# Weight stores moved from POOL to SP, half tiles without zero columns, twelve jobs with undivided scores, decay copies on ScalarE

## The chip, the core and the metric

The kernel runs on one core of one Trainium2 chip. The metric is device microseconds of one execution; the runs of the kernel before took 1110.32 to 1112.38 us, median 1110.91. The engines are TensorE (PE; its weight loads are shown as PEld), VectorE (DVE), ScalarE (ACT), GpSimd (POOL) and SyncE (SP), which issues most DMAs. Each engine works through its own queue in order.

## The reference

An attention with decay over 4 batches and 8 heads (576 positions, 64 columns per head), then two feed-forward layers (512 to 2048 to 512 columns) over the 2304 positions. Cut to what is computed:

```
scores = q @ k^T / sqrt(64)
cum    = cumsum(log(clip(f, 1e-4, 1)))
scores = where(causal, -1e9, scores + cum[:, None] - cum[None, :])
attn   = exp(scores - max) ; attn /= sum(attn) + 1e-9
x      = attn @ v                       # heads side by side: 2304 x 512
x      = (h * clip(h + 3, 0, 6) / 6) @ w_out1,  h = x @ w_in1
out    = where(h >= 1, h, where(h <= -1, 0, (h + 1)^2 / 4)) @ w_out2,  h = x @ w_in2
```

## The kernel before

The feed-forward layers go over 9 blocks of 256 positions per layer and 16 chunks of 128 hidden columns per block; one step of the list `steps` is one chunk of one block, 288 steps in all. `moe_h` makes the hidden columns of a step, `moe_o` (two steps later) adds them to the block's result in PSUM. Every operand is divided into a rounded part and a rest, and each product takes three matmuls.

Attention lies beside the first 112 steps. Its work is cut into jobs: 16 pairs of heads over the first 256 positions (kind "two", two heads in one job) and 16 pairs over the last 320 (two jobs of kind "one", one per head with two tiles of 128 rows, and one job "last": the half tiles of 64 rows of both heads, put together in one tile of 128). The jobs of three batches' first halves come first (12 jobs "two"). `u_load` issues a job's loads two jobs ahead (keys `kraw`, queries `qraw`, decay rows `dec`), `u_split` makes the masked decay `dm` on POOL and divides keys and queries, `u_scores` makes scores and softmax, `u_norm` and `u_trans` scale and transpose the probabilities, `u_out` multiplies by v. The first `NATS` = 8 jobs are taken undivided: their loads go straight into `kn` and `qn`, and each score is one f32 matmul. The first `DECS` = 3 jobs get their decay rows from a matmul in PSUM (`dc`) that is copied into `dec`.

Weights come as raw 64-bit words (`wraw`, four buffers). `w_split` takes half a chunk in five instructions: ScalarE's absolute value (line 175), then VectorE's lines 176, 180, 183 and 186 into `wr`. In layer 1 the result is divided into a resident buffer; for layer 2 (steps 38 to 106) it is stored to DRAM (`wf<-wr`, line 191, from POOL) for later. `wr` has two buffers, and the result of a finished block (`osb`, line 611) takes its buffers from the same tag.

The program is written in a planned order (`goal` from the costs in `seq`, `weights_until(g)` at each step); a scheduler then sets each engine's queue from priorities and an assumed timeline. In a tile pool a buffer is taken over when its last user is done; an instruction then waits at its place in the queue.

Of the kernel before, what the change touches and what calls it, by code (L numbers as in the profile page):

```python
# [16 lines left out]
P = 128  # L17
# [7 lines left out]
QA = 256  # L25
# [3 lines left out]
DECS = 3  # L29
NATS = 8  # L30
NORMS = 12
# [40 lines left out]
def tile_kernel(  # L72
# [88 lines left out]
    def w_split(kind, c, half, s, raw):  # L161
# [7 lines left out]
        ks = slice(4 * half, 4 * half + 4)  # L169
        r = moe.tile([P, 4, P], F32, tag="wr", name="wr", bufs=2)  # L170
        rf = r.rearrange("p k n -> p (k n)")
# [18 lines left out]
        if s is None:  # L190
            nc.gpsimd.dma_start(out=wf[c][:, ks], in_=r)
        else:
            rounded("a", wsb[s][:, 0, ks], r)
            rest("v", wsb[s][:, 1, ks], r, wsb[s][:, 0, ks])

    def w_keep(c, s):
# [31 lines left out]
    def u_load(n):  # L228
# [13 lines left out]
        if d["nat"]:  # L242

            kk = att.tile([P, S], F32, tag="kk", name="kn", bufs=3)
            qq = att.tile([P, 2 * QA], F32, tag="qh", name="qn", bufs=3)
            nc.sync.dma_start(out=kk[:, 0:nk], in_=k[b, h:h + 2, :, 0:nk].rearrange("h p n -> (h p) n"))
            for y in range(2):
                nc.sync.dma_start(
                    out=qq[y * D:(y + 1) * D, 0:nq], in_=q[b, h + y, y * D:(y + 1) * D, q0:q0 + nq]
                )  # L250
            d.update(kk=kk, qh=qq)
        else:
            kraw = att.tile([P, S], F32, tag="kraw", name="kraw", bufs=1)
            qraw = att.tile([P, 2 * QA], F32, tag="qraw", name="qraw", bufs=1)
            for y in range(2):
                nc.sync.dma_start(
                    out=kraw[y * D:(y + 1) * D, 0:nh * nk].rearrange("p (h n) -> p h n", h=nh),
                    in_=k[b, h:h + nh, :, 0:nk].rearrange("h p n -> p h n"),
                )
            if kind == "two":  # L260
                nc.sync.dma_start(
                    out=qraw.rearrange("p (h n) -> p h n", h=nh),
                    in_=q[b, h:h + nh, :, q0:q0 + nq].rearrange("h p n -> p h n"),
                )
            else:

                o = QA + W4 * (h % 2)
                nc.gpsimd.memset(qraw[:, S - o:S - o + W4], 0.0)
                nc.sync.dma_start(out=qraw[:, 0:QA], in_=q[b, h, :, q0:q0 + QA])
                nc.sync.dma_start(out=qraw[:, o:o + W4], in_=q[b, h, :, q0 + QA:S])  # L270
            d.update(kraw=kraw, qraw=qraw)
        w = nk if kind == "two" else 4 * P
        dec = att.tile([P, S], F32, tag="dec", name="dec")
        if n < DECS:
            t = bank("dc")
            for y in range(nh):
                ty = t[:, y * QA:(y + 1) * QA]
                for c in range(QA // P):
# [3 lines left out]
                    )  # L282
            rounded("v", dec[:, 0:nh * nk], t[:, 0:nh * nk])
        else:
# [8 lines left out]
    def u_split(n):  # L293
# [13 lines left out]
        else:  # L307
# [6 lines left out]
            if not d["nat"]:  # L314
# [4 lines left out]
                ql = att.tile([P, 2 * QA], F32R, tag="ql", name="ql", bufs=3)  # L319
                w, x = nh * d["nk"], 2 * QA if kind == "two" else QA + P  # L320
                rounded("a", kk[:, 0:w], kraw[:, 0:w])
# [8 lines left out]
    def softmax(d, z, py, pieces):  # L330

        mx, sm = d["mx"], d["sum"]
        for x, (s, dc, a, e) in enumerate(pieces):
            nc.vector.tensor_tensor_reduce(  # L334
                out=py[:, a:e], in0=s, in1=dc, scale=-0.125,
                scalar=mx[:, 2 * z:2 * z + 1] if x else 3.0e38,
                op0=ALU.add, op1=ALU.min, accum_out=mx[:, 2 * z + x:2 * z + x + 1],
            )
        x = len(pieces) - 1
# [4 lines left out]
    def u_scores(n, i):  # L344
# [5 lines left out]
        if kind == "last":  # L350
            pr = att.tile([P, S], F32, tag="prob2", name="prob2")
            d["prob"][i] = pr
            ta, tb = bank("sc"), bank("sc")
            for part in ("qh", "ql"):
                for t, a, e in ((ta, 0, 4 * P), (tb, 4 * P, S)):
                    for y in range(2):
                        o = jobs[n - 2 + y]
                        nc.tensor.matmul(
                            t[:, 0:e - a], lhsT=o[part][:, QA:QA + P], rhs=o["kk"][:, a:e],
                            start=part == "qh" and y == 0, stop=part == "ql" and y == 1,  # L360
                        )
            softmax(d, 0, pr, [(ta, dec[:, 0:4 * P], 0, 4 * P), (tb[:, 0:W4], dm[:, 0:W4], 4 * P, S)])
            return
# [23 lines left out]
        for y in range(nh):  # L387
            t, zd = ts[y], y * 2 + j
            pieces = [(t[:, 0:w0], dec[:, y * nk:y * nk + w0], 0, w0)] if w0 else []
            pieces.append((t[:, w0:width], dm[:, zd * P:(zd + 1) * P], w0, width))  # L390
            softmax(d, zd, pr[:, y * width:(y + 1) * width], pieces)
# [186 lines left out]
    def moe_o(g):  # L578
# [30 lines left out]
        if n == NCH - 1:  # L609
            for k in range(2):  # L610
                o = moe.tile([P, 512], F32, tag="wr", name="osb", bufs=2)
                scale = 1.0 / 6.0 if layer == 0 else 1.0
# [69 lines left out]
    for n, c in enumerate(first):  # L682
        t = PRE0 + (PRE1 - PRE0) * n // NCH
        wq += [(t - 3, t, "raw", c, half, None) for half in range(2)]
    wq.sort(key=lambda x: x[0])
# [7 lines left out]

    def weights_until(t):
        weights_ahead(t)
        while any(x[1] <= t for x, _ in pend):
# [9 lines left out]

    upper = att.tile([P, QA], F32, tag="upper", name="upper", bufs=1)
    nc.gpsimd.memset(upper, 1.0)
# [122 lines left out]
```

## Time and profile before

| | |
|---|---|
| median of 3 runs | 1110.91 us (1110.32 to 1112.38) |
| profiled execution | 1115.45 us, of which the span of instructions is 1113.7 us |
| busy in the span | PE 1048.2, PEld 947.3, DVE 635.4, ACT 512.6, POOL 138.4 us |
| mean granted TensorE clock | 0.964 of 2.4 GHz |
| instructions | 20349 |
| DMA | 144.35 MB, mean 130 GB/s |

Attention and the weight splits end near 557 us; what comes after is feed-forward work alone. A busy share over the whole span therefore mixes stages with different limits, and the rows below are cut by stage.

### The profile page before, as it was taken

The numbers are of one execution on the slowest core, as the hardware profiler recorded it, in microseconds if no ns is written. First come the engines' busy times: TensorE is split into PE (matmuls) and PEld (weight loads), VectorE is DVE, ScalarE is ACT, GpSimd is POOL, SyncE is SP. The second block draws the span as 40 slices with busy tenths as digits, with TensorE's granted clock in tenths as the row PEclk, the third lists the DMA queues.
The fourth block names the chain that finished last, engine by engine and source line by source line (L and its number), as shares of the span: only waits on it lengthen the run. The fifth ranks groups of instructions, "written<-read, shape, count | busy, mean of one in ns | idle before, by whom it ended". The sixth has DMA issues, their size and how long they took to land.

```text
span 1113.7 us, 20349 instructions
## 1 busy us (share of the span) xinstructions
PE 1048.2 (94%) x7324; PEld 947.3 (85%) x7324; DVE 635.4 (57%) x1846; ACT 512.6 (46%) x1314; POOL 138.4 (12%) x335
## 2 busy tenths in 40 slices
PE   7987998969889998989999999999999999999998
PEld 4676888958789888878889999998999999999997
DVE  8999984665677777767754336532333333333232
ACT  6876754545456654545554235432223323233232
POOL 2100000111111111111000000111211212212111
PEclk8697999989999999998999999999999999999999
DMA  8965781764496595774545125310100101000000
GB/s 253 314 212 175 218 272 57 221 219 121 128 339 189 152 325 162 231 262 128 182 151 185 39 65 182 97 38 1 39 10 29 39 1 39 20 19 29 1 21 19
DMA packets 72101, 144.35 MB, mean 130 GB/s; under 512 B 11840, under 2 KB 43072, under 8 KB 67904
## 3 DMA queue, kind: packets, MB, share of 16 engines
q1 hardware_dynamic: 69440, 134.66, 38.5%
q0 software_dynamic: 2560, 8.39, 1.9%
q8 instruction: 57, 0.93, 0.4%
q14 instruction: 44, 0.36, 0.1%
HBM read 116.74 MB, written 26.29 MB: 128 GB/s over the span
## 4 chain that ended last, share of the span: by engine, by line
PE 70%; DMA 14%; DVE 9%; issue 4%; ACT 2%; SPq 0%; POOL 0%; ACTq 0%; DVEq 0%; POOLq 0%
PE hp L552 31%; PE o L604 18%; PE o L597 12%; DMA dec<-ncum 5%; PE av L466 3%; PE pt L424 3%; DMA wf<-wr 2%; PE sc L383 2%; DMA qraw<-in_q 2%; DMA wraw<-in_w 2%; DVE prob L334 2%; DMA kraw<-in_k 1%; DMA x2d<-osb 1%; DMA w<-wf 1%; DVE wr L183 1%
## 5 line engine op out<-in xcount | busy, mean ns | idle before, releaser
L597 PE MATMUL o<-g,w 128*128 128x256 f32 x1728 | 254.1, 293 | 22.3 <-ACT g L118 18.8
L597 PEld LDWEIGHTS o<-g,w 128*128 128x128 f32 x1728 | 228.5, 195 | 31.9 <-ACT g L118 22.1
L552 PE MATMUL hp<-xt,w 128*128 128x256 f32 x1728 | 249.4, 291 | 4.9 <-ACT w L118 3.6
L552 PEld LDWEIGHTS hp<-x,w 128*128 128x128 f32 x1728 | 227.3, 191 | 12.8
L552 PEld LDWEIGHTS hp<-xt,w 128*128 128x128 f32 x1728 | 226.3, 194 | 11.3 <-ACT w L118 4.4
L552 PE MATMUL hp<-x,w 128*128 128x256 f32 x1728 | 231.8, 283 | 0.0
L604 PE MATMUL o<-w,g 128*128 128x512 f32 x864 | 224.9, 395 | 0.0
L126 DVE TENSOR_TENSOR g<-u,g 128x256 fp32r<-128x256 f32 x288 | 123.4, 430 | 106.0 <-POOL g L120 86.8
L561 ACT ACTIVATE u<-hp 128x256 f32<-128x256 f32 x144 | 55.4, 386 | 267.9 <-PE hp L552 264.9
L604 PEld LDWEIGHTS o<-w,g 128*128 128x128 f32 x864 | 152.6, 189 | 25.4
L563 DVE SCALAR_TENSOR_TENSOR u<-hp,u 128x256 f32<-128x256 f32 x144 | 60.7, 423 | 157.4 <-ACT u L562 157.4
L120 POOL TENSOR_SCALAR g<-u 128x256 fp32r<-128x256 f32 x144 | 58.7, 408 | 399.5 <-PE o L604 242.2
L340 ACT ACTIVATE prob<-prob,mx 128x256 f32<-128x256 f32 (+4 forms) x144 | 83.5, 581 | 35.9 <-DVE mx L334 35.2
L559 DVE SCALAR_TENSOR_TENSOR u<-u,hp 128x256 f32<-128x256 f32 x144 | 59.5, 416 | 57.2 <-ACT u L558 57.0
L558 ACT ACTIVATE u<-hp 128x256 f32<-128x256 f32 x144 | 54.0, 379 | 79.7 <-PE hp L552 79.1
L424 PE MATMUL pt<-ident,prob 128*128 128x128 f32 (+1 forms) x400 | 68.6, 292 | 22.4 <-DVE prob L409 18.2
L118 ACT ACTIVATE g<-u 128x256 fp32r<-128x256 f32 x144 | 59.0, 413 | 36.4 <-DVE u L559 35.7
L424 PEld LDWEIGHTS pt<-ident,prob 128*128 128x128 f32 (+1 forms) x400 | 49.1, 148 | 28.8 <-issue 11.4
L118 ACT ACTIVATE pt<-pt 128x512 f32<-128x512 f32 (+3 forms) x160 | 61.5, 433 | 22.1 <-PE pt L424 21.9
L175 ACT ACTIVATE wr<-wraw 128x512 f32<-128x512 f32 x64 | 43.2, 674 | 49.3 <-DMA wf<-wr 25.8
L334 DVE CUSTOM_DVE_ANT_0 prob<-sc,dec 128x128 f32<-128x128 f32 (+3 forms) x112 | 50.8, 457 | 24.6 <-PE sc L383 15.9
L562 ACT ACTIVATE u<-u 128x256 f32<-128x256 f32 x144 | 60.2, 420 | 4.4
(72 smaller groups left out, 954.0 us busy)
## 6 DMA issues: line engine op xcount, KB each, us to landing
wraw<-in_w SPq DMA_DIRECT2D x64, 512.0 KB, 9.7
w<-wf SPq DMA_DIRECT2D x24, 1024.0 KB, 8.9
dec<-ncum SPq DMA_DIRECT2D x45, 256.0 KB, 7.0
kraw<-in_k SPq DMA_DIRECT2D x64, 144.0 KB, 5.7
wf<-w SPq DMA_DIRECT2D x8, 1024.0 KB
wf<-wr POOLq DMA_DIRECT2D x32, 256.0 KB, 6.2
w<-wf SPq DMA_DIRECT2D x16, 512.0 KB, 3.5
vv<-in_v SPq DMA_DIRECT2D x16, 320.0 KB, 5.4
```

Source lines behind the costliest of these rows:

```text
L118: nc.scalar.activation(out=out, in_=in_, func=AF.Copy)
L120: nc.gpsimd.tensor_scalar(out=out, in0=in_, scalar1=1.0, scalar2=1.0, op0=ALU.mult, op1=ALU.mult)
L126: e.tensor_tensor(out=out, in0=in_, in1=hi.bitcast(F32), op=ALU.subtract)
L334: nc.vector.tensor_tensor_reduce(out=py[:, a:e], in0=s, in1=dc, scale=-0.125, scalar=mx[:, 2 * z:2 * z + 1] if x else 3.0e38, op0=ALU.add, ...
L340: nc.scalar.activation(out=py, in_=py, func=AF.Exp, scale=-1.0, bias=mx[:, 2 * z + x:2 * z + x + 1], accum_out=sm[:, z:z + 1],)
L424: nc.tensor.transpose(t[:nk, o:o + P], p[:, c:c + nk], ident)
L552: nc.tensor.matmul(hp, lhsT=ws[:, a, k], rhs=x[:, bb], start=(k == 0 and a == 0 and bb == 0), stop=(k == KD - 1 and bb == 1),)
L559: nc.vector.scalar_tensor_tensor(out=u, in0=u, scalar=6.0, in1=hp, op0=ALU.min, op1=ALU.mult)
L562: nc.scalar.activation(out=u, in_=u, func=AF.Square)
L563: nc.vector.scalar_tensor_tensor(out=u, in0=hp, scalar=1.0, in1=u, op0=ALU.max, op1=ALU.min)
L597: nc.tensor.matmul(o, lhsT=ws[:, a, KD + k], rhs=gg[:, bb], start=False, stop=(n == NCH - 1 and bb == 1 and k % 2 == 1),)
L604: nc.tensor.matmul(acc[j][k], lhsT=gg[:, bb, k * P:(k + 1) * P], rhs=ws[:, a, KD:2 * KD].rearrange("p k n -> p (k n)"), start=(n == 0 and ...
```

## The change

Stores of split weights are collected in a list and issued by SP at the start of the next step (`w_store`); the raw loads of layer 2 may go out six steps ahead of their split, not three; `wr` has three buffers. Twelve jobs are undivided, not eight. The copy of the decay rows from PSUM is ScalarE's. The queries of a job "one" are loaded in one piece of 320 columns; the zero columns that stood beside the half tiles, and POOL's memset for them, are gone. Instead the scores of the two half tiles are made in separate PSUM areas, the first with 64 rows, the second with 128 of which the upper 64 are used, in three banks, and the softmax's maximum pass runs once per half. The constant `upper` shares the buffer of `kraw`.

```
-NATS = 8
+NATS = 12
...
-        r = moe.tile([P, 4, P], F32, tag="wr", name="wr", bufs=2)
+        r = moe.tile([P, 4, P], F32, tag="wr", name="wr", bufs=3)
...
         if s is None:
-            nc.gpsimd.dma_start(out=wf[c][:, ks], in_=r)
+            stores.append((wf[c][:, ks], r))
...
+    def w_store():
+        for out_, r in stores:
+            nc.sync.dma_start(out=out_, in_=r)
+        stores.clear()
...
-            if kind == "two":
-                nc.sync.dma_start(
-                    out=qraw.rearrange("p (h n) -> p h n", h=nh),
-                    in_=q[b, h:h + nh, :, q0:q0 + nq].rearrange("h p n -> p h n"),
-                )
-            else:
-                o = QA + W4 * (h % 2)
-                nc.gpsimd.memset(qraw[:, S - o:S - o + W4], 0.0)
-                nc.sync.dma_start(out=qraw[:, 0:QA], in_=q[b, h, :, q0:q0 + QA])
-                nc.sync.dma_start(out=qraw[:, o:o + W4], in_=q[b, h, :, q0 + QA:S])
+            nc.sync.dma_start(
+                out=qraw[:, 0:nh * nq].rearrange("p (h n) -> p h n", h=nh),
+                in_=q[b, h:h + nh, :, q0:q0 + nq].rearrange("h p n -> p h n"),
+            )
...
-            rounded("v", dec[:, 0:nh * nk], t[:, 0:nh * nk])
+            rounded("a", dec[:, 0:nh * nk], t[:, 0:nh * nk])
...
-                w, x = nh * d["nk"], 2 * QA if kind == "two" else QA + P
+                w, x = nh * d["nk"], nh * d["nq"]
...
+        for x, piece in enumerate(pieces):
+            for s, dc, a, e, y in piece:
+                rs = slice(0, P) if y is None else slice(y * D, y * D + D)
+                nc.vector.tensor_tensor_reduce(
+                    out=py[rs, a:e], in0=s, in1=dc, scale=-0.125,
...
-            ta, tb = bank("sc"), bank("sc")
+            ta, tc_, tb = bank("sc"), bank("sc"), bank("sc")
+            tt = [[ta, tb[:, 0:W4]], [tc_, tb[:, P:P + W4]]]
+            for y in range(2):
+                o = jobs[n - 2 + y]
+                for part in ("qh", "ql"):
+                    for x, (a, e) in enumerate(((0, 4 * P), (4 * P, S))):
+                        m = D if y == 0 else P
                         nc.tensor.matmul(
-                            t[:, 0:e - a], lhsT=o[part][:, QA:QA + P], rhs=o["kk"][:, a:e],
+                            tt[y][x][:m, 0:e - a], lhsT=o[part][:, QA + W4 - m:QA + W4], rhs=o["kk"][:, a:e],
...
-        wq += [(t - 3, t, "raw", c, half, None) for half in range(2)]
+        wq += [(t - 6, t, "raw", c, half, None) for half in range(2)]
...
     def weights_until(t):
+        w_store()
         weights_ahead(t)
```

Where instructions now stand is shown at three places, all around the first stores of layer 2's weights. First POOL's queue before; `wf` is the store of a split, `dm<-dec` a mask over decay rows, `qraw` the memset of zero columns.

```order
L268 MEMSET qraw 128x64
L191 DMA wf_98<-wr 128x512
L299 AFFINE_SELECT dm<-dec 128x64
L303 AFFINE_SELECT dm<-dec 64x64
L191 DMA wf_98<-wr 128x512
L191 DMA wf_99<-wr 128x512
L309 AFFINE_SELECT dm<-dec 128x256
L268 MEMSET qraw 128x64
L191 DMA wf_99<-wr 128x512
```

POOL's queue now, in the same part of the program:

```order
L309 AFFINE_SELECT dm<-dec 128x256 x2
L299 AFFINE_SELECT dm<-dec 128x64
L303 AFFINE_SELECT dm<-dec 64x64
L309 AFFINE_SELECT dm<-dec 128x256 x2
L299 AFFINE_SELECT dm<-dec 128x64
L303 AFFINE_SELECT dm<-dec 64x64
```

The masks alone are left; before, the second store stood behind two masks, and masks behind stores. Second, SP's queue before at that place (`w<-wf` reloads a chunk's weights, `wraw` loads raw words):

```order
L618 DMA x2d<-osb 128x2x256 x2
L256 DMA kraw<-in_k 64x576 x2
L157 DMA w_118<-wf_85 128x2048
L236 DMA dec<-ncum 128x1x576
L223 DMA vv<-in_v 128x2x320
L154 DMA wraw<-in_w 128x1024 x2
L157 DMA w_117<-wf_84 128x2048
L285 DMA dec<-ncum 128x512
```

SP's queue now:

```order
L626 DMA x2d<-osb 128x2x256
L157 DMA w_118<-wf_85 128x2048
L200 DMA wf_98<-wr 128x512
L154 DMA wraw<-in_w 128x1024
L200 DMA wf_98<-wr 128x512
L154 DMA wraw<-in_w 128x1024
L243 DMA dec<-ncum 128x1x576
L230 DMA vv<-in_v 128x2x320
L200 DMA wf_99<-wr 128x512
L157 DMA w_117<-wf_84 128x2048
L154 DMA wraw<-in_w 128x1024
```

The stores stand each ahead of a raw load, and the decay rows have moved behind two such pairs. Third, ScalarE's queue before; the number behind `wr` tells one use of a buffer from another, and with two buffers `wr_3267` takes over that of `wr_2998`.

```order
L175 ACTIVATE wr_2998<-wraw_2785 128x512
L175 ACTIVATE wr_3005<-wraw_2787 128x512
L118 ACTIVATE g_2672<-u_2669 128x256
L340 ACTIVATE prob1_2678,sum_2560<-prob1_2678,mx_2561 128x512
L340 ACTIVATE prob0_2710,sum_2648<-prob0_2710,mx_2649 128x384
L558 ACTIVATE u_2743<-hp_2730 128x256
L118 ACTIVATE xt_2760<-av_2749 128x256
L118 ACTIVATE g_2746<-u_2743 128x256
L558 ACTIVATE u_2802<-hp_2789 128x256
L118 ACTIVATE xt_2763<-av_2749 128x64
L118 ACTIVATE g_2805<-u_2802 128x256
L175 ACTIVATE wr_3267<-wraw_3076 128x512
```

ScalarE's queue now; with three buffers, two of which last held a block's result (`osb`), `wr_3233` takes over that of `wr_2955`.

```order
L622 ACTIVATE osb_2669<-o1_1441 128x512
L175 ACTIVATE wr_2955<-wraw_2545 128x512
L175 ACTIVATE wr_2965<-wraw_2547 128x512
L342 ACTIVATE prob0_2592,sum_2520<-prob0_2592,mx_2521 128x384
L175 ACTIVATE wr_3225<-wraw_2793 128x512
L118 ACTIVATE pt_2409<-pt_2612 128x8x64
L566 ACTIVATE u_2631<-hp_2618 128x256
L566 ACTIVATE u_2705<-hp_2692 128x256
L118 ACTIVATE pt4_2410<-pt_2637 64x128
L118 ACTIVATE g_2634<-u_2631 128x256
L175 ACTIVATE wr_3233<-wraw_2961 128x512
```

Three splits stand directly behind the block's result, and the fourth, the first that waits for a store, has eight rows between it and the first; before, the third had ten.

## Rows read from the trace of the kernel before

**Rows 1.** The page: busy time of TensorE, its share of the span, instructions.

```profile
PE 1048.2 (94%) x7324; PEld 947.3 (85%) x7324; DVE 635.4 (57%) x1846; ACT 512.6 (46%) x1314; POOL 138.4 (12%) x335
```

**Rows 2.** Stretches: length, busy time of PE, PEld, DVE, ACT, POOL, clock, DMA, GB/s.

```profile
20.00:105.00 85.00, 71.67 (x433) 56.04 (x431) 81.93 (x267) 66.93 (x182) 7.09 (x10) 0.80 0.79 251
105.00:197.00 92.00, 83.88 (x641) 77.94 (x642) 68.09 (x202) 53.24 (x134) 4.82 (x14) 0.96 0.55 176
...
219.70:240.00 20.30, 10.11 (x68) 9.93 (x67) 9.91 (x30) 6.30 (x18) 3.06 (x7) 0.75 0.76 252
...
298.00:317.00 19.00, 12.38 (x67) 11.38 (x66) 12.77 (x38) 7.61 (x20) 3.24 (x8) 0.82 0.76 289
...
498.00:512.00 14.00, 9.89 (x47) 9.00 (x46) 10.31 (x30) 6.82 (x16) 3.66 (x9) 0.63 0.42 131
...
557.00:700.00 143.00, 143.00 (x1162) 137.06 (x1161) 69.20 (x172) 60.68 (x144) 5.79 (x16) 1.00 0.39 125
```

**Rows 3.** Waits, 197 to 557 us: who, for whom, total us, times, longest.

```profile
POOL dm L299 <- DMA dec<-ncum: 87.7, 9, 13.4
...
ACT wr L175 <- DMA wf<-wr: 25.8, 8, 7.6
...
ACT wr L175 <- DMA x2d<-osb: 11.3, 5, 5.1
```

**Rows 4.** ScalarE in order of time, 218.5 to 236 us: start, duration, [idle before].

```profile
219.37 0.42 ACT L118 ACTIVATE g<-u 128x256 fp32r<-128x256 f32 x1
227.37 0.66 ACT L175 ACTIVATE wr<-wraw 128x512 f32<-128x512 f32 x1 [7.57 <-DMA wf<-wr]
```

**Rows 5.** TensorE in order of time, 218.5 to 236 us.

```profile
221.22 2.08 PE L597 MATMUL o<-g,w 128*128 128x256 f32 x16
233.49 0.66 PE L424 MATMUL pt<-ident,prob 128*128 128x128 f32 x2 [10.19 <-DVE prob L409]
```

**Rows 6.** POOL in order of time, 205 to 232 us.

```profile
219.06 0.23 POOL L299 TENSOR_SCALAR_AFFINE_SELECT dm<-dec 128x64 f32<-128x64 f32 x1 [7.59 <-DMA dec<-ncum]
219.36 0.41 POOL L303 TENSOR_SCALAR_AFFINE_SELECT dm<-dec 64x64 f32<-64x64 f32 x1
219.73 0.56 POOL L191 DMA_DIRECT2D wf<-wr  x1
```

**Rows 7.** Waits of SP's queue, 197 to 557 us.

```profile
SPq L154 <- DVE wr L186: 45.0, 16, 9.2
```

**Rows 8.** DMA issues: out<-in, engine, count, KB each, median us to landing.

```profile
wf<-wr POOLq DMA_DIRECT2D x32, 256.0 KB, 6.2
...
x2d<-osb SPq DMA_DIRECT2D x18, 256.0 KB, 3.7
```

**Rows 9.** Groups by shape, VectorE, 20 to 105 us: count | busy us, mean ns.

```profile
L126 DVE TENSOR_TENSOR kk<-kraw,kk 64x512 fp32r<-64x512 f32 x4 | 2.8, 690 | 0.1
L126 DVE TENSOR_TENSOR ql<-qraw,qh 128x512 fp32r<-128x512 f32 x4 | 2.7, 687 | 0.0
```

**Rows 10.** Groups by shape, whole span, VectorE and ScalarE.

```profile
L118 ACT ACTIVATE pt<-pt 128x512 f32<-128x512 f32 x64 | 37.8, 592 | 16.8 <-PE pt L424 16.6
...
L334 DVE DVE_READ_ACCUMULATOR2_ANT mx<- 128x1 f32 x256 | 21.0, 82 | 0.0
...
L126 DVE TENSOR_TENSOR ql<-qraw,qh 128x384 fp32r<-128x384 f32 x32 | 17.9, 560 | 15.8 <-ACT qh L118 15.6
...
L334 DVE CUSTOM_DVE_ANT_0 prob<-sc,dec 128x512 f32<-128x512 f32 x16 | 11.0, 687 | 7.8 <-DMA dec<-ncum 6.6 <-PE sc L358 1.1
...
L334 DVE CUSTOM_DVE_ANT_0 prob<-sc,dm,mx 128x64 f32<-128x64 f32 x16 | 4.5, 279 | 0.3 <-PE sc L358 0.2
...
L122 DVE COPY dec<-dc 128x512 f32<-128x512 f32 x3 | 2.1, 685 | 1.4 <-PE dc L279 1.4
```

**Rows 11.** Groups by shape, whole span, TensorE.

```profile
L373 PE MATMUL sc<-kn,qn 64*128 64x256 f32 x32 | 11.2, 533 | 1.6 <-ACT pt L118 0.8 <-DVE mx L334 0.7
...
L383 PE MATMUL sc<-kk,qh 128*128 128x256 f32 x16 | 4.6, 308 | 0.0
```

More of the change, by code (lines that the diff above doesn't have):

```diff
@@ L194, in w_split @@
             rest("v", wsb[s][:, 1, ks], r, wsb[s][:, 0, ks])
+    stores = []
+    def w_store():
+        for out_, r in stores:
+            nc.sync.dma_start(out=out_, in_=r)
+        stores.clear()
     def w_keep(c, s):
@@ L332, in softmax @@
         mx, sm = d["mx"], d["sum"]
[L333 to L338, printed above, removed]
+        for x, piece in enumerate(pieces):
[3 more added lines that the diff above has]
+                    out=py[rs, a:e], in0=s, in1=dc, scale=-0.125,
+                    scalar=mx[rs, 2 * z:2 * z + 1] if x else 3.0e38,
+                    op0=ALU.add, op1=ALU.min, accum_out=mx[rs, 2 * z + x:2 * z + x + 1],
+                )
         x = len(pieces) - 1
@@ L352, in u_scores @@
             d["prob"][i] = pr
-            ta, tb = bank("sc"), bank("sc")
[L354 to L357, printed above, removed]
+            ta, tc_, tb = bank("sc"), bank("sc"), bank("sc")
[5 more added lines that the diff above has]
+                        m = D if y == 0 else P
                         nc.tensor.matmul(
-                            t[:, 0:e - a], lhsT=o[part][:, QA:QA + P], rhs=o["kk"][:, a:e],
-                            start=part == "qh" and y == 0, stop=part == "ql" and y == 1,
-                        )
-            softmax(d, 0, pr, [(ta, dec[:, 0:4 * P], 0, 4 * P), (tb[:, 0:W4], dm[:, 0:W4], 4 * P, S)])
+                            tt[y][x][:m, 0:e - a], lhsT=o[part][:, QA + W4 - m:QA + W4], rhs=o["kk"][:, a:e],
+                            start=part == "qh", stop=part == "ql",
+                        )
+            softmax(d, 0, pr, [
+                [(tt[y][0][y * D:y * D + D], dec[y * D:y * D + D, 0:4 * P], 0, 4 * P, y) for y in range(2)],
+                [(tt[y][1][y * D:y * D + D], dm[y * D:y * D + D, 0:W4], 4 * P, S, y) for y in range(2)],
+            ])
             return
@@ L388, in u_scores @@
             t, zd = ts[y], y * 2 + j
-            pieces = [(t[:, 0:w0], dec[:, y * nk:y * nk + w0], 0, w0)] if w0 else []
-            pieces.append((t[:, w0:width], dm[:, zd * P:(zd + 1) * P], w0, width))
+            pieces = [[(t[:, 0:w0], dec[:, y * nk:y * nk + w0], 0, w0, None)]] if w0 else []
+            pieces.append([(t[:, w0:width], dm[:, zd * P:(zd + 1) * P], w0, width, None)])
             softmax(d, zd, pr[:, y * width:(y + 1) * width], pieces)
@@ L610, in moe_o @@
             for k in range(2):
-                o = moe.tile([P, 512], F32, tag="wr", name="osb", bufs=2)
+                o = moe.tile([P, 512], F32, tag="wr", name="osb", bufs=3)
                 scale = 1.0 / 6.0 if layer == 0 else 1.0
@@ L704, in tile_kernel @@
     lf = att.tile([P, L], F32, tag="prob1", name="lf")
-    upper = att.tile([P, QA], F32, tag="upper", name="upper", bufs=1)
+    upper = att.tile([P, QA], F32, tag="kraw", name="upper", bufs=1)
     nc.gpsimd.memset(upper, 1.0)
```

## The prediction

> **What bounds the kernel now.** I read the stages first, then the waits, then the order of time inside the worst stretch. TensorE is busy for 94% of the span [rows 1], and from 557 us on it hardly pauses (143.00 of 143.00 us in 557:700 [rows 2]), so nothing that the change touches (attention and weight splits, all done by then) can be won there. What can be won lies before. From 20 to 105 us VectorE is the limit: 81.93 of 85 us busy against TensorE's 71.67. After that TensorE is the limit in most stretches, with holes: in the three stretches 219.7:240, 298:317 and 498:512 it is busy for 10.11 of 20.30, 12.38 of 19.00 and 9.89 of 14.00 us [rows 2]. That is 10.2 + 6.6 + 4.1 = 20.9 us of idle in 53 us, and the granted clock there is 0.75, 0.82 and 0.63, which is a mix of its two levels, 1.2 and 2.4 GHz.
>
> The waits say what they have in common [rows 3]: the first ScalarE instruction of a weight split (L175) waits for a store `wf<-wr` to land, 8 times, 25.8 us; for the store of a finished block, which shares the `wr` buffers, 5 times, 11.3 us. ScalarE runs in order, so everything behind stands too. In the worst case ScalarE stands for 7.57 us [rows 4], and TensorE follows with 10.19 us of idle [rows 5]. POOL's rows say why that store was late: it sat behind an `affine_select` that waited 7.59 us for decay rows, went out at 219.73 and freed its buffer only at 227.4 [rows 4, 6]. So the buffer is held by POOL's order as much as by the transfer.
>
> **Part 1: stores on SP, three `wr` buffers, raw loads six steps ahead.** Removed: 32 store issues from POOL and the dependence of a store on a decay transfer. Added: 32 issues on SP. They stand directly ahead of raw loads that SP already held for the same VectorE instruction (L186: 16 waits, 45.0 us [rows 7]), so the added wait mostly replaces one; what is queued behind a waiting store is a raw load, then weight reloads and decay rows. A buffer is now needed again three splits later, not two. The earlier raw loads remove nothing large, since no row of the worst waits is a wait for a raw load in this part; I set them at 0.
> Bounds: at best the three stretches lose all idle, 20.9 us, and what the low clock took, at most (1 - 0.75) x 20.30 + (1 - 0.82) x 19.00 + (1 - 0.63) x 14.00 = 13.7 us, together 34.6 us. At worst 0, if the waits move to SP's stores. My value: the first stretch goes whole, 10.2 + 5.1 = 15.3 us, since its cause is POOL's order. Of the other two, half: they also hold the wait for the block's own store, which stays. (6.6 + 3.4 + 4.1 + 5.2) / 2 = 9.7 us. Gain 25 us.
> Against it: the new ScalarE order has the splits no further apart than before (the fourth of a group needs the first one's store eight rows of the order after it was begun), so short waits stay. A store of this size took 6.2 us from POOL, and one of the same size from SP 3.7 us [rows 8]. I take the difference, 2.5 us, once for each of the five groups of splits, 12.5 us of ScalarE, half of it reaching TensorE: +6 us. Bounds 0 and the 25.8 us of now.
> A rule that speaks against this part: the Trainium skill, "DMA: Bandwidth & Descriptors", section "Queues, rings and completion order", says that a DMA engine takes turns between queue rows and works through one row's ring in order, so a store that leaves POOL's row for SP's loses its own turn and starts behind all that SP has issued. The trace so far points the other way, with 3.7 us from SP against 6.2 us from POOL [rows 8]; what the rule would make of the time is the first rival.
>
> **Part 2: twelve jobs undivided, decay rows by ScalarE.** Four jobs lose both VectorE splits, 4 x 690 + 4 x 687 ns = 5.5 us, all eight inside 20:105 [rows 9], and three copies of 685 ns leave VectorE, 2.1 us [rows 10]. Sum 7.6 us on the engine that is 96% busy there. TensorE has 13.3 us of idle in that stretch, so the gain is not capped by it; but it and ScalarE (66.93 of 85 us) are close behind, so I take 5 us. Bounds 0 (the next engine takes it all) and 7.6. The three copies cost ScalarE about 592 ns each [rows 10], beside the splits it loses; 0. TensorE swaps eight divided matmuls per job for four undivided ones, which last 533 ns for 256 columns against 308 for each of the two divided parts [rows 11]: 0, as two times 308 is no less; bounds -1 and +1 us over four jobs. Undivided scores take one bank per head; cover is the idle of TensorE just named, and without it I would add 1 us.
>
> **Part 3: half tiles without zero columns.** POOL loses 32 memsets, SP one of two query loads in each of 32 jobs, and the query splits 64 of 384 columns: VectorE 560 ns each now [rows 10], at most 32 x 560 x 64/384 = 3 us less. The price is in the softmax: each of the 16 tiles now makes four passes of 64 partitions where it made two of 128. A pass costs by its columns, not its partitions: `kk` on 64 partitions with 512 columns takes 690 ns, `ql` on 128 takes 687 [rows 9]. So 687 + 279 + 2 x 82 ns = 1.13 us more per tile [rows 10], 16 x 1.13 = 18.1 us on VectorE, between 105 and 557 us. VectorE is busy for 74% of 105:197 [rows 2], so about a quarter of it should show: (18.1 - 3) / 4 = +4 us. Bounds -3 and 18.1. These tiles also hold three score banks for longer, and the next matmul group that turns to such a bank waits. No row shows it; bounds 0 and one pass more per tile, 16 x 0.69 = 11 us; I take 2.
>
> **Part 4: SP's order.** Decay rows and key loads now stand behind stores and earlier raw loads. They wait for VectorE instructions of about the same place, so I take +2 us; bounds 0 and the third rival's price.
>
> **Sum.** -25 + 6 - 5 + 4 + 2 + 2 = -16 us. The profiled execution took 1115.45 us (span 1113.7), so about 1099.5 there. It lies 4.5 us above the median 1110.91 of the runs, so the median should come to 1095 us.
>
> **Rivals.**
> First, the stalls move: the store leaves SP promptly but lands late behind loads. With two 1 MB reloads queued and 252 GB/s in 219.7:240 [rows 2], a store lands some 8 us after its issue, more than the 7.57 us that ScalarE stood. For it: the splits stay as dense. Against it: 3.7 us [rows 8], and the third buffer. Part 1 is then worth some 5 us instead of 19: 1109 us.
> Second, the stalls go whole: 34.6 instead of 25 and no new short waits, -16 - 10 - 6 = -32 us: 1079 us. For it: 25.8 us is the whole sum of those waits. Against it: the 11.3 us for the block's store remain.
> Third, on the other side, the decay rows. POOL already waits for them 87.7 us in nine places [rows 3]. There are 16 decay loads for half tiles; if each starts behind one store and one raw load more, 768 KB at 252 GB/s, it is 3.0 us later, 48 us in all. The rest of the sum without part 4 is -18 us, so this decides from the point where three eighths of the 48 us reach TensorE; with half of it the time is -18 + 24 = +6 us, median 1117 us. For it: the new order of SP has two stores and two raw loads between a weight reload and the decay load behind it. Against it: a wait of POOL for decay rows is mostly not one of TensorE, and stores and decay loads wait for VectorE instructions that are few rows apart.
> That the change does not do what it says is excluded for the stores: the new order of POOL holds none.
>
> **How the numbers follow.** Forecast (1087 to 1104) 0.55, first rival (1104 to 1112) 0.16, second (1075 to 1087) 0.15, third (1113 to 1125) 0.14. About 0.2%, 2.2 us, is what a measurement can tell from no change, so "same" is 1108.7 to 1113.1: some half of the first rival, 0.08. Faster 0.78, slower 0.14. The range that leaves out the deeper half of the second rival and most of the third is 1079 to 1114.
>
> **What would show it.** Right: `wf<-wr` no longer ends waits of L175 for more than some 12 us in all; no TensorE idle of 10 us near 220; VectorE about 10 us busier in all (18.1 - 7.6, less the narrower splits), its busy time to 105 us less by 7.6; POOL without stores. Wrong in part 1: waits of ScalarE for the stores stay above 20 us, or TensorE's clock falls in as many stretches. Wrong in part 3: TensorE waits for VectorE's `prob` or for banks in the half tiles. Wrong in part 4: decay transfers end TensorE's idle for more than now. The prediction is wrong if the stages before 557 us do not shrink by 8 us or more.

## The result, and the profile after

The changed kernel takes 1124.72 us (median of 4 runs, 1123.12 to 1129.93), the kernel before in the same comparison 1111.64 us (1110.32 to 1113.37): a ratio of 1.0114, 95% interval 1.0082 to 1.0145. It is slower by some 13 us where the prediction had it faster by 16, and the range up to 1114 us does not hold it. The profiled execution took 1124.15 us, its span is 1122.4 us.

The page of the changed kernel answers to [rows 1]:

```profile
PE 1047.4 (93%) x7324; PEld 942.2 (84%) x7324; DVE 644.9 (57%) x1899; ACT 508.9 (45%) x1309; POOL 114.8 (10%) x271
```

TensorE's work is the same, and so is the mean granted clock (0.964 in both profiled executions), so what grew is its idle time: 1113.7 - 1048.2 = 65.5 us before, 1122.4 - 1047.4 = 75.0 us now. VectorE has 9.5 us more, about as forecast. Then the stretches of [rows 2], in the same columns, though the program now stands elsewhere in them:

```profile
20.00:105.00 85.00, 63.17 (x361) 48.83 (x362) 77.09 (x250) 59.00 (x159) 5.61 (x7) 0.74 0.75 244
105.00:197.00 92.00, 90.61 (x704) 81.67 (x703) 67.30 (x211) 56.00 (x152) 4.32 (x10) 1.00 0.53 171
219.70:240.00 20.30, 14.71 (x101) 13.67 (x100) 12.43 (x39) 7.80 (x22) 0.88 (x3) 0.92 0.97 332
298.00:317.00 19.00, 16.22 (x107) 14.45 (x106) 16.12 (x51) 9.93 (x25) 0.61 (x1) 0.82 0.99 373
498.00:512.00 14.00, 14.00 (x115) 13.59 (x114) 9.82 (x33) 7.17 (x19) 1.47 (x4) 1.00 0.49 137
557.00:700.00 143.00, 139.80 (x1125) 132.57 (x1125) 70.66 (x193) 59.01 (x145) 6.21 (x16) 1.00 0.39 128
```

In the three stretches where the prediction saw the gain, TensorE is busy for 14.71, 16.22 and 14.00 us instead of 10.11, 12.38 and 9.89: 12.5 us less idle. It was lost again elsewhere, some of it already in 20:105 (63.17 us against 71.67). Attention does not end near 557 us in either kernel, as the text ahead of the prediction and the prediction have it: its last product `av` ends at 603.0 us before and at 612.5 us now. Only the weight splits are done by then (550.7 and 552.8 us). The waits from 197 to 557 us, in the columns of [rows 3]:

```profile
POOL dm L299 <- DMA dec<-ncum: 159.0, 11, 19.5
...
ACT wr L175 <- DMA wf<-wr: 26.0, 11, 7.4
...
ACT wr L175 <- DMA x2d<-osb: 7.9, 5, 2.5
```

The splits wait for stores as long as before: 26.0 us against 25.8, in 11 waits instead of 8. The longest stands at the same place as in [rows 4]. Here is ScalarE's row of it in the changed kernel, and then SP's rows ahead of it (start, duration, instruction):

```profile
217.81 0.42 ACT L118 ACTIVATE g<-u 128x256 fp32r<-128x256 f32 x1
225.65 0.66 ACT L175 ACTIVATE wr<-wraw 128x512 f32<-128x512 f32 x1 [7.42 <-DMA wf<-wr]
```

```profile
210.70 0.40 SPq L154 DMA_DIRECT2D wraw<-in_w  x1
211.20 0.55 SPq L243 DMA_DIRECT2D dec<-ncum  x1
212.89 0.38 SPq L230 DMA_DIRECT2D vv<-in_v  x1
216.41 0.33 SPq L200 DMA_DIRECT2D wf<-wr  x1
216.82 0.38 SPq L157 DMA_DIRECT2D w<-wf  x1
```

Before, the store went out late, at 219.73 [rows 6]. Now it goes out at 216.41, and its buffer comes free 9.2 us after that, where it was 7.6 us (219.73 to 227.37). The DMA engines are busy for 0.97 of the stretch. The store stopped waiting on POOL and takes longer to land instead. TensorE's rows show what is left of the hole of 10.19 us [rows 5]:

```profile
222.97 1.20 PE L605 MATMUL o<-g,w 128*128 128x256 f32 x8
228.23 2.17 PE L560 MATMUL hp<-xt,w 128*128 128x256 f32 x9 [4.06 <-DVE u L567]
```

The DMA issues of the changed kernel, in the columns of [rows 8]:

```profile
wraw<-in_w SPq DMA_DIRECT2D x64, 512.0 KB, 8.7
...
wf<-wr SPq DMA_DIRECT2D x32, 256.0 KB, 7.5
...
x2d<-osb SPq DMA_DIRECT2D x18, 256.0 KB, 4.0
```

A store from SP lands after 7.5 us in the median, from POOL it was 6.2 [rows 8]. The kernels of the experiments below agree: 7.3 to 10.1 us in all that store from SP, 5.4 to 6.5 us in all that store from POOL. Last, VectorE's groups by shape over the whole span, which answer to [rows 10]:

```profile
L336 DVE CUSTOM_DVE_ANT_0 prob<-sc,dec 64x512 f32<-64x512 f32 x32 | 22.0, 687 | 9.7 <-DMA dec<-ncum 4.5 <-PE sc L363 4.2
...
L126 DVE TENSOR_TENSOR ql<-qraw,qh 128x320 fp32r<-128x320 f32 x32 | 15.6, 487 | 5.6 <-ACT qh L118 5.2
...
L336 DVE CUSTOM_DVE_ANT_0 prob<-sc,dm,mx 64x64 f32<-64x64 f32 x32 | 9.0, 282 | 1.8 <-issue 0.6 <-PE sc L363 0.3
...
L336 DVE DVE_READ_ACCUMULATOR2_ANT mx<- 64x1 f32 x64 | 5.0, 78 | 0.0
```

The half tiles' passes take 22.0 + 9.0 + 5.0 = 36.0 us, against 11.0 + 4.5 + 32 x 0.082 = 18.1 us before: 17.9 us more. The query splits save 2.3 us.

### The profile page after: what moved, and what is told of

Its sections match the earlier page's. It is cut to its first block, busy times and chain, and to the rows that moved or that the text cites. A ratio compares the mean times of both kernels' runs of the same rounds, so it can differ in the third digit from the quotient of the medians.

```text
span 1122.4 us, 20224 instructions
## 1 busy us (share of the span) xinstructions
PE 1047.4 (93%) x7324; PEld 942.2 (84%) x7324; DVE 644.9 (57%) x1899; ACT 508.9 (45%) x1309; POOL 114.8 (10%) x271
## 4 chain that ended last, share of the span: by engine, by line
PE 73%; DMA 11%; DVE 10%; issue 3%; ACT 2%; SPq 1%; POOL 0%; DVEq 0%; ACTq 0%; POOLq 0%
PE hp L560 33%; PE o L612 18%; PE o L605 13%; PE av L474 3%; PE pt L432 3%; DMA dec<-ncum 3%; DMA wraw<-in_w 2%; DMA wf<-wr 2%; DVE prob L336 2%; PE sc L391 2%; DMA kraw<-in_k 1%; DVE wr L186 1%; DVE wr L183 1%; PE sc L363 1%; DMA qraw<-in_q 1%
## 5 line engine op out<-in xcount | busy, mean ns | idle before, releaser
L605 PE MATMUL o<-g,w 128*128 128x256 f32 x1728 | 248.0, 288 | 19.8 <-ACT g L118 11.4
L605 PEld LDWEIGHTS o<-g,w 128*128 128x128 f32 x1728 | 223.4, 190 | 30.7 <-ACT g L118 13.7
L342 ACT ACTIVATE prob<-prob,mx 128x128 f32<-128x128 f32 (+4 forms) x144 | 83.4, 580 | 45.4 <-DVE mx L336 44.9
L336 DVE CUSTOM_DVE_ANT_0 prob<-sc,dec 128x384 f32<-128x384 f32 (+3 forms) x128 | 61.6, 486 | 28.1 <-PE sc L391 16.6
L175 ACT ACTIVATE wr<-wraw 128x512 f32<-128x512 f32 x64 | 42.7, 671 | 58.6 <-DMA wf<-wr 26.0
L309 POOL TENSOR_SCALAR_AFFINE_SELECT dm<-dec 128x256 f32<-128x256 f32 (+1 forms) x48 | 29.5, 615 | 327.4 <-DMA dec<-ncum 167.6
```

What stands on the lines that cost most here:

```text
L336: nc.vector.tensor_tensor_reduce(out=py[rs, a:e], in0=s, in1=dc, scale=-0.125, scalar=mx[rs, 2 * z:2 * z + 1] if x else 3.0e38, op0=ALU.ad ...
L342: nc.scalar.activation(out=py, in_=py, func=AF.Exp, scale=-1.0, bias=mx[:, 2 * z + x:2 * z + x + 1], accum_out=sm[:, z:z + 1],)
L605: nc.tensor.matmul(o, lhsT=ws[:, a, KD + k], rhs=gg[:, bb], start=False, stop=(n == NCH - 1 and bb == 1 and k % 2 == 1),)
```

## The experiments

Each kernel was timed beside the kernel before on the same chip; a ratio is to those runs, with its 95% interval. "Step 0" and "step 90" are the starts of the hidden products of those steps in the profile, less those of the kernel before (44.3 and 495.5 us); "end" is the same for step 144, behind all attention. The table is worked out from the traces, the columns on VectorE (busy us) and on L175 (us of waits for stores `wf`, and for raw words; the same instruction is L181 in a_s3 and h_s3) are read from them.

| kernel | median us | ratio | VectorE | L175 | step 0 | step 90 | end |
|---|---|---|---|---|---|---|---|
| changed | 1124.72 | 1.0114 [1.0082, 1.0145] | 644.9 | 26.0, 13.1 | +9.0 | +12.3 | +9.4 |
| b_half | 1114.0 | 1.0008 [0.9983, 1.0032] | 650.7 | 20.7, 6.7 | +2.1 | -2.2 | +0.2 |
| b_stores | 1111.02 | 0.998 [0.9957, 1.0002] | 636.0 | 25.2, 17.0 | +9.0 | +6.3 | -1.2 |
| b_nats_dec | 1111.28 | 0.9967 [0.9945, 0.999] | 627.4 | 26.4, 2.4 | +0.6 | -5.9 | -7.8 |
| b_upper | 1112.8 | 1.0001 [0.9969, 1.0034] | 635.3 | 26.5, 4.5 | -0.7 | +0.6 | -1.0 |
| a_nohalf | 1109.08 | 0.996 [0.9937, 0.9984] | 630.2 | 29.4, 9.8 | +8.5 | +0.6 | -3.4 |
| p_sh | 1118.24 | 1.0056 [1.0035, 1.0077] | 650.3 | 25.9, 14.8 | +8.7 | +6.9 | +2.2 |
| p_hn | 1115.4 | 1.0031 [1.0009, 1.0052] | 644.2 | 22.7, 2.5 | +1.1 | -2.2 | +2.0 |
| a_s3 | 1125.36 | 1.0137 [1.0094, 1.018] | 644.9 | 26.1, 11.7 | -0.8 | +9.6 | +10.7 |
| a_passes | 1124.91 | 1.0095 [1.0066, 1.0125] | 645.6 | 26.6, 12.4 | +11.0 | +16.2 | +11.7 |
| a_half2 | 1105.99 | 0.9926 [0.9899, 0.9954] | 626.7 | 22.7, 13.8 | +9.6 | -2.1 | -9.4 |
| b_nd_half2 | 1100.93 | 0.9889 [0.9859, 0.992] | 627.7 | 25.5, 2.1 | +1.5 | -6.7 | -14.8 |
| h_w | 1104.14 | 0.9921 [0.9898, 0.9944] | 627.0 | 19.8, 2.1 | +0.9 | -10.1 | -13.1 |
| h_pool3 | 1110.09 | 0.9966 [0.9947, 0.9984] | 627.9 | 15.8, 13.7 | +10.1 | -0.1 | -4.8 |
| h_s3 | 1104.07 | 0.9917 [0.9884, 0.9949] | 627.4 | 14.9, 10.2 | -0.9 | -7.9 | -14.3 |

### One part alone on the kernel before

b_half has the half tiles without zero columns and nothing else of the change, in its core:

```
-            ta, tb = bank("sc"), bank("sc")
+            ta, tc_, tb = bank("sc"), bank("sc"), bank("sc")
...
+            for s, dc, a, e, y in piece:
+                rs = slice(0, P) if y is None else slice(y * D, y * D + D)
```

> The kernel before with the half tiles' edit alone (queries in one piece, no zero columns, three banks, four passes of 64 partitions). Theory A (each edit has its own price, and this one is the dear one): VectorE 15 to 16 us busier than 635.4, time +8 to +12 us, 1119 to 1123. Rival B (an edit's price is that of the new queue orders, not of its work): anywhere within 1100 to 1125, with the loss not where the half tiles are. If VectorE is as much busier and the time is within 3 us of before, the passes are hidden and the loss of the whole change is elsewhere.

b_stores has the stores on SP, three buffers, the raw loads six steps ahead, and `upper` in another buffer:

```
-            nc.gpsimd.dma_start(out=wf[c][:, ks], in_=r)
+            stores.append((wf[c][:, ks], r))
...
-        wq += [(t - 3, t, "raw", c, half, None) for half in range(2)]
+        wq += [(t - 6, t, "raw", c, half, None) for half in range(2)]
```

> The kernel before with the weight stores' edit alone (SP a step later, three wr buffers, raw loads six steps ahead, upper in kraw's buffer). Theory A: the stretch from step 30 to step 54 gains 8 to 10 us as in the changed kernel, the start loses 2 to 5 us because a third split now stands before the first exponentials; 1102 to 1108. Rival C (the third buffer at the start is the whole loss): step 0 late by 7 us or more, time above 1112.

b_nats_dec is two lines:

```
-NATS = 8
+NATS = 12
...
-            rounded("v", dec[:, 0:nh * nk], t[:, 0:nh * nk])
+            rounded("a", dec[:, 0:nh * nk], t[:, 0:nh * nk])
```

> The kernel before with twelve undivided jobs and ScalarE's decay copies alone. Theory A: VectorE 7.6 us less busy, time 1104 to 1110. Rival D (these two slow the start, as the copies stand behind splits that wait for raw words): step 0 late by 5 us or more, time 1115 to 1122.

b_upper is the smallest edit of the change, as a measure of what no change looks like:

```
-    upper = att.tile([P, QA], F32, tag="upper", name="upper", bufs=1)
+    upper = att.tile([P, QA], F32, tag="kraw", name="upper", bufs=1)
```

> The kernel before with one constant (upper) in another buffer, which costs no engine any work. Theory A: within 3 us of before, 1108 to 1114. Rival B: 4 us or more away from before in either direction, since the scheduler makes another order of it.

No part alone makes the kernel slower by more than can be told from no change: +0.1%, -0.2%, -0.3% and 0.0%. Their sum would be about -0.4%, and all of them together are +1.1%. So the loss is not in one part; it appears when the parts stand together. b_half came out as the last sentence of its expectation has it: VectorE is 15.3 us busier and the time is within 3 us of before. b_stores was outside both of its ranges, and b_nats_dec just above its theory's.

The stores' part, which was to bring 19 us, brings some 2, which cannot be told from none. The two waits of the splits in b_stores go with that:

```profile
ACT wr L175 <- DMA wf<-wr: 25.2, 9, 7.1
ACT wr L175 <- DMA wraw<-in_w: 17.0, 8, 4.4
```

The waits for stores are unchanged, and waits for raw words, 4.8 us in the kernel before, have come on top.

### The change without one part, and two parts together

a_nohalf is the changed kernel with the half tiles as they were:

```
-                w, x = nh * d["nk"], nh * d["nq"]
+                w, x = nh * d["nk"], 2 * QA if kind == "two" else QA + P
...
-            ta, tc_, tb = bank("sc"), bank("sc"), bank("sc")
+            ta, tb = bank("sc"), bank("sc")
```

p_sh is the kernel before with the edits of b_stores and b_half, p_hn with those of b_nats_dec and b_half.

> The changed kernel without the half tiles' edit: the stores' edit and the twelve jobs with ScalarE's copies together. Alone these two were 0.998 and 0.997 of before. Theory A (the loss is stores and half tiles meeting: more VectorE work ahead of each store and each buffer): 1103 to 1109. Rival B (stores and the twelve jobs meet at the start, where the third split waits for raw words and the relief of VectorE is worth nothing): step 12 late by 7 us or more, 1112 to 1120.

> Stores' edit and half tiles' edit on the kernel before, eight undivided jobs, VectorE's copies. Theory A: 1119 to 1126, as the changed kernel. Rival B: the sum of the two alone, 1110 to 1114.

> Half tiles' edit and the twelve jobs with ScalarE's copies on the kernel before, stores from POOL as before. Theory A and rival B: no part of this pair meets the stores, so the sum of the two alone, 0.9975, 1108 to 1112. If it is above 1115, the loss lies between these two and the stores are innocent.

Without the half tiles the change is faster than before (0.996). The half tiles are +0.1% on the kernel before, 1.0056 - 0.998 = +0.8% beside the stores' edit, 1.0031 - 0.9967 = +0.6% beside the other edits, and 1.0114 - 0.996 = +1.5%, about 17 us, beside both. So what the half tiles cost depends on the edits beside them, also on the stores' edit, which alone makes nothing faster. The two pairs answered to neither of their theories: p_sh lies between its two ranges, and p_hn, expected at the sum of its parts, is above 1115 us, so the half tiles cost something without the stores' move too.

### The start

The changed kernel reaches step 0 9.0 us late. With three buffers, three splits stand on ScalarE ahead of the first exponentials, and the third waits for raw words. The rows of ScalarE up to the table load in front of those exponentials (start, duration, instruction, idle before), in the kernel before and then in the changed one:

```profile
9.71 0.68 ACT L175 ACTIVATE wr<-wraw 128x512 f32<-128x512 f32 x1 [0.59 <-DMA wraw<-in_w]
10.41 1.28 ACT L340 ACT_TABLE_LOAD   x1
```

```profile
11.93 0.69 ACT L175 ACTIVATE wr<-wraw 128x512 f32<-128x512 f32 x1 [0.88 <-DMA wraw<-in_w]
12.63 1.28 ACT L342 ACT_TABLE_LOAD   x1
```

The exponentials begin 2.2 us later, and more such waits follow. a_s3 lets only every third stored split use the third buffer:

```
-        r = moe.tile([P, 4, P], F32, tag="wr", name="wr", bufs=3)
+        turns[0] += s is None
+        if s is None and turns[0] % 3 == 0:
+            r = moe.tile([P, 4, P], F32, tag="ws", name="wr", bufs=1)
+        else:
+            r = moe.tile([P, 4, P], F32, tag="wr", name="wr", bufs=2)
```

> The changed kernel, in which the third buffer is used by every third stored split alone: layer 1's splits and the block results turn over two, as before. Expected by the trace: no third split ahead of the first exponentials, step 0 within 2 us of before (changed: 9.0 late), waits of L175 for raw words to 105 us under 6 us (13.1). If what is late at the start stays late: 1110 to 1116. Rival (the start is slack that is regained by step 54 whatever it is): above 1119.

Step 0 is on time (-0.8 us), and the kernel ends as late as the changed one (+10.7 against +9.4). The start is no cause of the loss here: its 9 us are slack that the next steps give back (at step 30 the changed kernel is 1.9 us late, at step 54 it is 7.4 us early).

### What of the half tiles costs: passes, or banks and order

a_passes has the half tiles of the kernel before, zero columns and two banks, and differs from a_nohalf in the softmax alone:

```
-            softmax(d, 0, pr, [(ta, dec[:, 0:4 * P], 0, 4 * P), (tb[:, 0:W4], dm[:, 0:W4], 4 * P, S)])
+            softmax(d, 0, pr, [
+                [(ta[y * D:y * D + D], dec[y * D:y * D + D, 0:4 * P], 0, 4 * P, y) for y in range(2)],
+                [(tb[y * D:y * D + D, 0:W4], dm[y * D:y * D + D, 0:W4], 4 * P, S, y) for y in range(2)],
+            ])
```

> The changed kernel with the half tiles as they were (zero columns, two banks, one accumulation over both jobs), and only the softmax's minimum done in four passes over 64 partitions where there were two over 128: the added passes alone. Theory A (VectorE's passes are the price): VectorE's busy time rises from 630.2 to some 648 us, and the time from 1109 to 1122 to 1127 us, at or above the changed kernel's 1124.7. Rival C (the price is the third bank that each half tile holds, so that others' scores wait for a bank): the time stays within 1107 to 1114 us although VectorE has the passes.

a_half2 keeps the zero columns away but makes the second job's scores first, over 128 rows, and then the first job's over rows 0 to 63 of the same bank, so that one pass reads both:

```
-            ta, tc_, tb = bank("sc"), bank("sc"), bank("sc")
-            tt = [[ta, tb[:, 0:W4]], [tc_, tb[:, P:P + W4]]]
-            for y in range(2):
+            ta, tb = bank("sc"), bank("sc")
+            for y in (1, 0):
                 o = jobs[n - 2 + y]
+                m = P if y else D
...
+            softmax(d, 0, pr, [(ta, dec[:, 0:4 * P], 0, 4 * P), (tb[:, 0:W4], dm[:, 0:W4], 4 * P, S)])
```

> The changed kernel with its half tiles made in another order: the second job's product first, over all 128 rows, then the first job's over rows 0 to 63 of the same two banks, so that the zero columns are still gone but VectorE takes each piece in one pass over 128 partitions, and a tile holds two banks. Theory A (what the half tiles cost is VectorE's added passes): VectorE's busy time falls from 644.9 to some 627 us (630.2 without the half-tile edit, less the shorter low part), and the time comes to 1105 to 1111 us, near the 1109 of the kernel without the half-tile edit. Rival B (the cost is TensorE's order, y outside and part inside, or the missing zero columns' transfers): VectorE falls as much, but the time stays above 1118 us.

b_nd_half2 has the same half tiles on the kernel before, with twelve undivided jobs and ScalarE's copies, the stores left on POOL and the raw loads three steps ahead; against a_half2 it has

```
-        r = moe.tile([P, 4, P], F32, tag="wr", name="wr", bufs=3)
+        r = moe.tile([P, 4, P], F32, tag="wr", name="wr", bufs=2)
...
-            stores.append((wf[c][:, ks], r))
+            nc.gpsimd.dma_start(out=wf[c][:, ks], in_=r)
```

> The kernel before with three of the edits: twelve undivided jobs, decay rows copied by ScalarE, and half tiles without zero columns in one pass over 128 partitions (second job first, first job over it); stores stay on POOL with two buffers. Theory A: VectorE some 624 us (627.4 without the half tiles), and the time 1106 to 1110 us, ratio to before 0.993 to 0.998, below both kernels; the stores' move adds nothing that this one lacks. Rival D (the stores' move is worth something once VectorE has room): this one is over 2 us slower than the changed kernel with one-pass half tiles.

The three settle which part of the half tiles is dear. The passes alone put the changed kernel's time back: 1124.91 us, 1.0095 - 0.996 = +1.35%, 15 us, for 645.6 - 630.2 = 15.4 us more on VectorE. There is no third bank in it. Without the passes the change is 1105.99 us, below both kernels. One thing comes with the passes and was not tried apart: the scheduler gives every engine another order for them (of TensorE's 7324 matmuls in a_passes some 330 stand elsewhere than in a_nohalf). Here are VectorE's groups for the half tiles, first of a_half2, then of a_passes:

```profile
L334 DVE CUSTOM_DVE_ANT_0 prob<-sc,dec 128x512 f32<-128x512 f32 x16 | 11.0, 686 | 6.5 <-DMA dec<-ncum 5.8 <-PE sc L359 0.4
L334 DVE CUSTOM_DVE_ANT_0 prob<-sc,dm,mx 128x64 f32<-128x64 f32 x16 | 4.5, 279 | 0.3
```

```profile
L343 DVE CUSTOM_DVE_ANT_0 prob<-sc,dec 64x512 f32<-64x512 f32 x32 | 22.0, 687 | 6.4 <-DMA dec<-ncum 4.9 <-PE sc L367 0.8
L343 DVE CUSTOM_DVE_ANT_0 prob<-sc,dm,mx 64x64 f32<-64x64 f32 x32 | 9.1, 283 | 1.0
```

The same work is in twice as many instructions of the same length. The next two fences take the steps 54 to 90, where the changed kernel loses most; first its row of the stretch, then that of a_half2 (columns as in [rows 2]):

```profile
315.90:507.80 191.90, 169.04 (x1253) 152.37 (x1250) 141.70 (x459) 102.36 (x279) 12.18 (x26) 0.94 0.66 212
```

```profile
312.60:493.40 180.80, 165.78 (x1252) 149.53 (x1249) 131.21 (x428) 100.35 (x275) 11.35 (x26) 0.96 0.70 226
```

VectorE has 10.5 us more to do in the same steps, and the steps take 11.1 us longer, though VectorE is busy for only 74% of them. TensorE's idle grows from 15.0 to 22.9 us. The two differences are near each other, but not one and the same: 6.5 of the 10.5 us are on the line of the minimum passes, the rest is other work that another order has put there, and between a_nohalf and a_passes the same steps take 9.9 us longer for 5.0 us on VectorE. Nor is all that the changed kernel loses there due to the passes: the kernel before takes 172.2 us for these steps, and a_half2, 10.7 us early at step 54, is 8.6 us slower in them too.

Which waits of TensorE grew? Over the whole of a_nohalf, and then of a_passes (who waits for whom, total us, times, longest), these are the two largest:

```profile
PE pt L431 <- DVE prob L416: 28.5, 11, 6.5
PE o L604 <- ACT g L118: 9.2, 8, 4.1
```

```profile
PE o L609 <- ACT g L118: 20.6, 10, 8.6
PE pt L436 <- DVE prob L421: 17.4, 6, 5.1
```

All of TensorE's waits together grew from 57.2 to 70.5 us. The waits for attention's probabilities became shorter, those for the feed-forward block's own `g` longer. So the loss does not show where the passes' result is used. The chain of work that ended last does not single VectorE out either: its share is 10% in the changed kernel and 7% in a_half2, but 10% in a_nohalf, which has no added pass, and 9% in a_passes.

And b_nd_half2, with no store moved at all, is the fastest of all: 1100.93 us, 0.9889, some 5 us below what its theory gave it. The next question was therefore what the stores' edit costs once VectorE has room.

### The stores' edit by parts

h_w and h_pool3 stand on b_nd_half2. h_w has the move of the stores to SP alone, two buffers, raw loads three steps ahead. h_pool3 has three buffers and raw loads six steps ahead, stores from POOL (and `upper` in the buffer of `kraw`, which alone was worth 0.0%). h_s3 is a_half2 with the buffers of a_s3. First h_w's core, then h_pool3's, against b_nd_half2:

```
-            nc.gpsimd.dma_start(out=wf[c][:, ks], in_=r)
+            stores.append((wf[c][:, ks], r))
```

```
-        r = moe.tile([P, 4, P], F32, tag="wr", name="wr", bufs=2)
+        r = moe.tile([P, 4, P], F32, tag="wr", name="wr", bufs=3)
...
-        wq += [(t - 3, t, "raw", c, half, None) for half in range(2)]
+        wq += [(t - 6, t, "raw", c, half, None) for half in range(2)]
```

> The kernel before with twelve undivided jobs, decay rows copied by ScalarE and one-pass half tiles, and of the edit of the stores only their move to SP a step later; two wr buffers, raw loads at three steps. Theory S (the move to SP is what the stores' edit costs, since a store lands later there and keeps a split waiting longer with only two buffers): 1105 to 1112 us, and ScalarE's splits wait 30 us or more for stores. Rival T (the start is what it costs, since a third split goes ahead of the first exponentials): the start is as before, and the time 1099 to 1103 us.

> The same kernel with stores from POOL as before, but with three wr buffers and the raw loads at six steps. Theory S: the start loses its 8 us by step 0 and regains them later; 1098 to 1102 us, with the splits' waits for stores under 20 us. Rival T (the third split at the start is the price): 1104 to 1108 us, as much as the changed kernel with one-pass half tiles.

> The changed kernel with one-pass half tiles, the third wr buffer used by every third stored split alone, so that step 0 comes on time. Theory S: the start's loss is regained anyway, so 1104 to 1108 us, as without this edit. Rival T: 1098 to 1102 us, as much as with stores from POOL.

Neither theory had h_w or h_pool3, and h_s3 lies at the edge of the first one's range. The move to SP (h_w, 0.9921) is at most a little slower than POOL's stores (0.9889; the intervals overlap), and the splits did not wait longer for stores: 19.8 us against 25.5. The third buffer with the early raw loads (h_pool3, 0.9966, interval 0.9947 to 0.9984, apart from 0.9859 to 0.992) costs some 9 us, though it shortens those waits most, to 15.8 us. Its two waits of L175:

```profile
ACT wr L175 <- DMA wf<-wr: 15.8, 4, 9.2
ACT wr L175 <- DMA wraw<-in_w: 13.7, 8, 2.8
```

What the stores no longer hold up, raw words do, and 10.1 us are lost by step 0. h_s3 repairs step 0, and both waits are shorter than in a_half2 (14.9 and 10.2 us against 22.7 and 13.8), from which it differs by the buffers alone. Yet the two cannot be told apart (0.9917 and 0.9926). Its runs lie between 1098.29 and 1108.87 us. So with stores from SP the late start costs nothing that was measured; whether it is what h_pool3 loses is open, as the buffers and the raw loads were not tried apart there.

## Why the prediction was wrong

**Part 1** is its largest failed term: -19 us forecast, -0.2% or 2 us measured alone. The step "the first stretch goes whole, since its cause is POOL's order" was half the cause. POOL's order did go, and the hole at 220 us shrank from 10.19 to 4.06 us. But the other half, the transfer, grew: 9.2 us from issue to a free buffer, not 7.6, in a stretch whose DMA share is 0.97. The store's price on SP was taken from `x2d`, 3.7 us [rows 8]. It measured 7.5 us, and `x2d` is still at 4.0, so the landing time of one line was no price for another of its size on its queue; what makes the two differ was not tried. The prediction's test, no more than some 12 us of waits, failed with 26.0 us. The gain from the clock, counted in at 5.1 us and half of 8.6, did not come either, not in the whole: the mean granted clock is unchanged. And "The earlier raw loads remove nothing large ... I set them at 0" looked only at what they remove: waits for raw words went from 4.8 to 17.0 us in b_stores, and with three buffers and early loads h_pool3 is 9 us slower than b_nd_half2. The store that lands late is the first rival's mechanism, with a chance of 0.16; that rival gave part 1 some 5 us. The Trainium skill, "DMA: Bandwidth & Descriptors", section "Queues, rings and completion order", has a row's ring worked off in order; by that rule a store which leaves POOL's row starts behind what SP has issued, and the 7.5 us against 6.2 agree with it. The later landing alone does not give the time: with the stores on SP the splits of h_w waited less for them, 19.8 us against 25.5.

**Part 2** held: -5 us forecast, 0.9967 measured, 3.7 us, with VectorE 8.0 us less busy where 7.6 were forecast.

**Part 3** decided the sign. Its gross term was right: 18.1 us forecast, 17.9 us in the rows. The step that failed is "VectorE is busy for 74% of 105:197, so about a quarter of it should show". Beside the other edits the passes cost as much as they are busy, 15 us for 15.4 us (a_passes against a_nohalf), not a quarter of it, and on the kernel before the whole part, passes and gain together, costs nothing that can be told (b_half, +0.1%). So the busy share of an engine set the price in neither case: it says how often the engine is idle, not whether a given instruction stands in a chain. A half tile's passes lie between its scores and its exponentials, and behind them on the same engine lie the block's own `u` and `g` and the splits; the longer waits of TensorE for `g` fit that. Why the price is full in one kernel and mostly hidden in another stays open; the passes alone on the kernel before were not tried, and b_half also holds the gain named below. That the other edits use up the idle time that hides it is not shown: TensorE's idle in a_nohalf, 1109.8 - 1047.8 = 62.0 us, is near the 65.5 us of before. Nor is the work of the passes parted from the new order of the queues. The two microseconds for the third bank are not needed: a_passes has none and is as slow. No run has that bank without the passes.

What the part also holds, and the prediction put at no more than 3 us of VectorE, is a gain. With the passes taken back, no zero columns are worth 0.9967 - 0.9889 = 0.8%, 9 us, with the stores on POOL (b_nats_dec to b_nd_half2). Beside the stores' edit it is 0.996 - 0.9926 = 0.3%, less than the intervals tell apart. One load, a memset of POOL and 64 columns of each split go, and the half tiles' products come in another order; which of them it is was not tried.

**Part 4** was +2. POOL's wait for decay rows at half tiles went from 87.7 to 159.0 us, yet POOL waits, not TensorE. Over the whole execution that wait is as long in a_half2, which is below the time before; here are the rows of the changed kernel and then of a_half2:

```profile
POOL dm L299 <- DMA dec<-ncum: 217.5, 15, 19.5
```

```profile
POOL dm L299 <- DMA dec<-ncum: 225.2, 16, 18.1
```

In the chain of work that ended last, decay rows have 4.9% before and 2.7% in the changed kernel. So the result lies in the third rival's range (1113 to 1125, chance 0.14), but by luck: its mechanism was not the cause.

**The sum.** With measured terms: stores -2, undivided jobs and copies -4, half tiles +17 beside both, together +11, against the 13 measured. The 17 us are the changed kernel less a_nohalf, so this sum tests only that stores, jobs and copies together are worth what they are alone.

## What to carry to other kernels

Do not price added instructions by the engine's busy share. Here the passes cost their whole busy time beside two other edits, while the edit that holds them cost +0.1% on the kernel before; if they lie between a product and its consumer, let the range reach to the full price, and measure them beside the edits that they will ship with. When a buffer waits for a store, ask how long the transfer will take after its issue has been moved: here an issue 3.3 us earlier, with the DMA engines busy for 0.97, shortened ScalarE's wait only from 7.57 to 7.42 us. Take a change apart before it is dropped: three of its edits with one pass instead of two were 1.1% faster than the kernel before.

## What was not expected of the hardware

A pass over 64 partitions and 512 columns took 687 ns, one over 128 partitions 686: half the rows save nothing, as the rows of the splits had said already [rows 9]. A product over rows 0 to 63 into a PSUM bank whose 128 rows hold another finished product leaves rows 64 to 127 as they were, so that both halves can be read in one pass (a_half2, which has 16 passes of 128x512 where a_passes has 32 of 64x512). And 256 KB from one queue took 4.0 us as `x2d` and 7.5 us as `wf` in one execution.
